# Linear attention (hedgehog) plus dense Mish branch on one core: the first group's layer norm by single tiles, both weight folds ahead of the keys

## The chip, the cores and the metric

One core of a Trainium2 chip runs the whole program in one launch. The metric is device time in microseconds (us), the median of several executions. Besides these, one execution was recorded by the hardware profiler; all rows below are of that one.

## The reference

The input `x` (2048 tokens of 512 numbers, bf16) is layer-normalised, and two branches of the result are added to it:

```python
xn = _layernorm(x)                                  # (x - mean) / sqrt(var + 1e-5)
# A: 32 heads of 16, feature map by two softmaxes
q, k, v = split(xn @ wqkv)
pq, pk = q @ w_phi[h], k @ w_phi[h]
phi_q = concat(softmax(pq), softmax(-pq)); phi_k = concat(softmax(pk), softmax(-pk))
o = (phi_q @ (phi_k.T @ v)) / (phi_q @ sum(phi_k) + 1e-6)
A = o @ wo
# B: dense layer with Mish, F = 1792
h = xn @ w1 + b1
B = (h * tanh(softplus(h))) @ w2
out = x + A + B
```

## The kernel before

The tokens are worked through in four groups of 512, each of four tiles of 128 tokens. The first loop (L445 to L463) does for each group: keys and values (`stage_kv_pair`, two tiles of tokens at a time), queries (`stage_q`), the layer norm of the *next* group (`stage_ln`), the sum of phi_k times v over the tokens (`stage_kvacc`), and the first dense layer with Mish (`stage_h`). A second loop (L479) does the attention output and the second dense layer with the projection.

`stage_ln` takes a group's four tiles on VectorE: statistics (`bn_stats`, `bn_aggr`, L169 and L170), one square root for all four on ScalarE (L171), one reciprocal (L172), four normalising passes to `xn` (L176). TensorE then transposes 16 blocks (L191) into two PSUM tiles `ptr`, and ScalarE copies each to `xnT` (L196).

`fold(src, dst)` multiplies w_phi into the key or query weights ahead of time, so that `pk` and `pq` need one product each. It transposes 16 blocks of the raw weights into PSUM (`ptrw`, L217), ScalarE copies them to `wT` (L223, two buffers), TensorE multiplies with the block-diagonal `Wbd` into four PSUM tiles `pf` (L228), and VectorE casts each to `wkp` or `wqp` (L235). The keys are folded before the group loop; the queries are folded in the first pass of the loop, between the first group's keys and values and its queries (L449).

PSUM is split into three pools: `big` (tag kq, two tiles of two banks: pk, pq, ph, pnd), `bank_v` (two banks: pv, pf, po) and `bank_m` (two banks: ptr, ptrw, pb, pS, pkv, ptro). Buffers of a tag go round: a tile waits until an older one has been read.

The order on each engine is not that of the source: a planner in the framework orders the instructions at build time, by their place in the source and by when it believes them to be ready. `chain` (L139) adds edges that keep ScalarE's Sqrt, Exp and Mish calls in source order, so that the activation tables are switched a fixed number of times. At run time each engine works strictly in that built order. DMAs are issued from the queues of SyncE (SP) and ScalarE (ACT).

Of the kernel before, what the change touches and what calls it, by code (L numbers as in the profile page):

```python
# [8 lines left out]
BF16 = mybir.dt.bfloat16  # L9
FP32 = mybir.dt.float32  # L10

ACT = mybir.ActivationFunctionType
ALU = mybir.AluOpType
# [4 lines left out]
def kernel(  # L18
# [12 lines left out]
    nc = tc.nc  # L31
    P = 128
    S, D, NH, DH, F = 2048, 512, 32, 16, 1792
    NG = 4
    TPG = 4
    NT = NG * TPG
    KT = D // P
# [3 lines left out]
    x2 = A_x.flatten_outer_dims()  # L41
    x_g = x2.rearrange("(g t p) d -> g p t d", t=TPG, p=P)
    x_t = x2.rearrange("(n p) d -> n p d", p=P)
# [4 lines left out]
    w1_v = B_w1.rearrange("(kt p) c -> p kt c", p=P)  # L48
    w2_v = B_w2.rearrange("(ft p) c -> p ft c", p=P)
    wphi_v = A_w_phi.rearrange("(j i) a b -> (i a) j b", j=4)  # L50
    b1_v = B_b1.rearrange("(f p) -> f p", p=P)

    consts = ctx.enter_context(tc.tile_pool(name="consts", bufs=1))
# [5 lines left out]
    xnpool = ctx.enter_context(tc.tile_pool(name="xn", bufs=4))  # L59
    xnTpool = ctx.enter_context(tc.tile_pool(name="xnT", bufs=2))  # L60
    spool = ctx.enter_context(tc.tile_pool(name="small", bufs=4))
# [5 lines left out]
    prep_w = tc.alloc_tile_pool(name="prep_w", bufs=1)  # L67
    xgs = [None] * NG
    xgs[0] = xpool.tile([P, TPG, D], BF16, name="xg")
    for t in range(TPG):  # L70
        nc.sync.dma_start(xgs[0][:, t, :], x_t[t])
    wk_raw = prep_w.tile([P, KT, D], BF16, name="wk_raw")
    nc.scalar.dma_start(wk_raw[:], wqkv_v[:, :, D : 2 * D])
    Wsrc = prep_w.tile([P, 4, DH], BF16, name="Wsrc")
    with nc.allow_non_contiguous_dma(reason="tiny w_phi load"):
        nc.scalar.dma_start(Wsrc[:], wphi_v)
# [2 lines left out]
    wq_raw = prep_w.tile([P, KT, D], BF16, name="wq_raw")  # L79
    nc.scalar.dma_start(wq_raw[:], wqkv_v[:, :, 0:D])  # L80
    b1row = prep_w.tile([FT, P], BF16, name="b1row")
    nc.scalar.dma_start(b1row[:], b1_v)
    w1_sb = wts.tile([P, KT, F], BF16, name="w1_sb")
    nc.sync.dma_start(w1_sb[:, :, 0 : F // 2], w1_v[:, :, 0 : F // 2])
    nc.sync.dma_start(w1_sb[:, :, F // 2 : F], w1_v[:, :, F // 2 : F])
    xgs[1] = xpool.tile([P, TPG, D], BF16, name="xg")
    nc.sync.dma_start(xgs[1][:], x_g[1])
    w2_sb = wts.tile([P, FT, D], BF16, name="w2_sb")
# [5 lines left out]
    ident = consts.tile([P, P], BF16, name="ident")  # L94
    make_identity(nc, ident[:])
    eps_t = consts.tile([P, 1], FP32, name="eps_t")
    nc.gpsimd.memset(eps_t[:], 1e-5)

    mask17 = consts.tile([P, 8, VW], FP32, name="mask17")
    nc.gpsimd.memset(mask17[:], 1.0)  # L100
# [1 line left out]
        out=mask17[:],  # L102
# [8 lines left out]
        out=mask17[:],  # L111
# [13 lines left out]
    wqp = wts.tile([P, KT, D], BF16, name="wqp")  # L125
# [13 lines left out]
    def chain(ins):  # L139

        prev = last_of.get("act")
        last_of["act"] = ins
        if prev is not None:
            tc.add_manual_dep(
                ins.ins,
                prev.ins.name,
                mybir.DependencyInfo(
                    mybir.DependencyClass.NoSync, mybir.DependencyReason.DATA
                ),
                reason="table order",  # L150
            )
# [4 lines left out]
    def bank_v(name):  # L156
        return ps_v.tile([P, 512], FP32, name=name, tag="v")

    def bank_m(name, shape=None, dt=FP32):
        return ps_m.tile(shape or [P, 512], dt, name=name, tag="m")  # L160


    def stage_ln(g):
        xg = xgs[g]
        mv = spool.tile([P, TPG, nc.vector.BN_AGGR_DIM], FP32, name="mv")
        rstd = spool.tile([P, TPG], FP32, name="rstd")
        for t in range(TPG):
            st = spool.tile([P, nc.vector.BN_STATS_DIM], FP32, name="st")
            nc.vector.bn_stats(st[:], xg[:, t, :])  # L169
            nc.vector.bn_aggr(mv[:, t, :], st[:])  # L170
        chain(nc.scalar.activation(rstd[:], mv[:, :, 1], ACT.Sqrt, bias=eps_t[:]))  # L171
        nc.vector.reciprocal(rstd[:], rstd[:])  # L172
        xns = []
        for t in range(TPG):
            xn = xnpool.tile([P, D], BF16, name="xn")
            nc.vector.tensor_scalar(  # L176
                out=xn[:],
                in0=xg[:, t, :],
                scalar1=mv[:, t, 0:1],
                scalar2=rstd[:, t : t + 1],  # L180
                op0=ALU.subtract,
                op1=ALU.mult,
            )
            xns.append(xn)
        xnT = xnTpool.tile([P, KT, 512], BF16, name="xnT")
        for kh in range(2):
            ptr = bank_m("ptr", [P, 2, 512], BF16)
            for t in range(TPG):
                for k in range(2):
                    kt = 2 * kh + k  # L190
                    nc.tensor.transpose(  # L191
                        ptr[:, k, t * P : (t + 1) * P],
                        xns[t][:, kt * P : (kt + 1) * P],
                        ident[:],
                    )
            nc.scalar.copy(xnT[:, 2 * kh : 2 * kh + 2, :], ptr[:])  # L196
        return xnT


# [2 lines left out]
        out=Wbd[:].rearrange("p j (i e) -> p j i e", e=DH),  # L202
        in0=B16b[:, None, :]
# [6 lines left out]
    def fold(src, dst):  # L210
        wTs = []
        for jh in range(2):
            ptr = bank_m("ptrw", [P, 2, 512], BF16)
            for jj in range(2):
                j = 2 * jh + jj
                for kt in range(KT):
                    nc.tensor.transpose(  # L217
                        ptr[:, jj, kt * P : (kt + 1) * P],
                        src[:, kt, j * P : (j + 1) * P],
                        ident[:],  # L220
                    )
            wT = prep_w.tile([P, 2, 512], BF16, name="wT", bufs=2)
            nc.scalar.copy(wT[:], ptr[:])  # L223
            wTs.append(wT)
        for kt in range(KT):
            pf = bank_v("pf")
            for j in range(4):
                nc.tensor.matmul(  # L228
                    pf[:, j * P : (j + 1) * P],
                    lhsT=wTs[j // 2][:, j % 2, kt * P : (kt + 1) * P],  # L230
                    rhs=Wbd[:, j, :],
                    start=True,
                    stop=True,
                )
            nc.vector.tensor_copy(dst[:, kt, :], pf[:])  # L235


    def stage_kv_pair(xnT, pr):
# [47 lines left out]
    def stage_kvacc(g, parts):  # L286
        for s0, s1 in ((0, 3), (3, 6), (6, 8)):
            n = s1 - s0
            pkv = bank_m("pkv", [P, n, 8 * VW])
            for s in range(s0, s1):  # L290
                pl, j = divmod(s, 4)
                for t in range(TPG):
                    ek, v12s = parts[t // 2]
                    nc.tensor.matmul(  # L294
                        pkv[:, s - s0, :],
                        lhsT=ek[:, pl, t % 2, j * P : (j + 1) * P],
                        rhs=v12s[t % 2][:, pl, 8 * j : 8 * j + 8, :],
                        start=(t == 0),
                        stop=(t == TPG - 1),
                    )  # L300
            if g == 0:
                nc.vector.tensor_copy(kvacc[:, s0:s1, :], pkv[:])
            else:
                nc.vector.tensor_tensor(
                    out=kvacc[:, s0:s1, :],
                    in0=pkv[:],
                    in1=kvacc[:, s0:s1, :],
                    op=ALU.add,
                )
# [127 lines left out]

    xnTs = [None] * NG
    acts = [None] * NG
    xnTs[0] = stage_ln(0)  # L440
    fold(wk_raw, wkp)
    pb = bank_m("pb", [P, FT], BF16)
    nc.tensor.transpose(pb[:], b1row[:], ident[0:FT, 0:FT])
    nc.vector.tensor_copy(b1f[:], pb[:])
    for g in range(NG):  # L445
        xnT = xnTs[g]
        parts = [stage_kv_pair(xnT, pr) for pr in range(2)]
        if g == 0:
            fold(wq_raw, wqp)  # L449
            prep_w.release()  # L450
            apool3 = ctx.enter_context(tc.tile_pool(name="act3", bufs=1))
            oTpool = ctx.enter_context(tc.tile_pool(name="oT", bufs=2))
            rpool = ctx.enter_context(tc.tile_pool(name="rden", bufs=4))
            opool = ctx.enter_context(tc.tile_pool(name="o_t", bufs=4))
            ypool = ctx.enter_context(tc.tile_pool(name="y", bufs=2))
        stage_q(g, xnT)
        if g + 1 < NG:
            if g + 1 > 1:
                xgs[g + 1] = xpool.tile([P, TPG, D], BF16, name="xg")
                nc.sync.dma_start(xgs[g + 1][:], x_g[g + 1])  # L460
            xnTs[g + 1] = stage_ln(g + 1)
        stage_kvacc(g, parts)
        acts[g] = stage_h(xnT, apool if g + 1 < NG else apool3)  # L463
# [3 lines left out]
        out=kvv[:, 0:4, :, DH],  # L467
        in0=kvv[:, 0:4, :, DH],
        scalar1=1e-6,
        scalar2=None,  # L470
        op0=ALU.add,
    )
    nc.vector.tensor_tensor(
        out=kvm[:].rearrange("p s (h v) -> p s h v", v=VW),
        in0=kvv,
# [36 lines left out]
```

## Time and profile before

| what | value |
|---|---|
| median of 3 runs | 224.42 us (224.35 to 227.0) |
| the profiled execution, its own time | 226.06 us |
| its span, first to last instruction | 224.3 us |
| TensorE (PE) busy | 197.7 us, 88% |
| VectorE (DVE) busy | 120.4 us, 54% |
| ScalarE (ACT) busy | 101.2 us, 45% |
| mean granted TensorE clock | 0.985 of full |

The span is what the trace covers; the profiled execution's own time is 1.76 us longer than it, and 1.64 us above the median of the runs. An engine's share of busy time is an average over stages that have different limits, so it is to be read stage by stage.

### The profile page before, as it was taken

The page shows a single profiled execution, that of the slowest core. Times are in us where ns is not written, and L with a number is a line of the kernel's source. Part 1 is how long each engine was busy: PE and PEld are TensorE (multiplying, and loading weights), DVE is VectorE, ACT ScalarE, POOL GpSimd, SP SyncE. Part 2 cuts the span into 40 slices and gives each one's busy share as a digit, 9 for nine tenths or more (in the row PEclk, how much of TensorE's full clock was granted, in tenths as well). Part 3 has the DMA queues.
Part 4 walks back from the last instruction along what each step waited for, and adds up shares of the span by engine and source line. Part 5 has one row for each costly group of instructions (what it writes and reads, how often), then busy time and mean ns, then how long its engine had stood idle before and what let it go on. Part 6 is the DMA issues. An engine that isn't in the chain of part 4 may idle for free.

```text
span 224.3 us, 2903 instructions
## 1 busy us (share of the span) xinstructions
PE 197.7 (88%) x1185; PEld 100.1 (45%) x1185; DVE 120.4 (54%) x205; ACT 101.2 (45%) x124; POOL 8.6 (4%) x26
## 2 busy tenths in 40 slices
PE   0089455889999999999999999999999999999993
PEld 0066113346444356443464345564464455446441
DVE  1627598695229992199930998562263145218121
ACT  0263800595789847799469874423003003000200
POOL 2000011000001100011000110000000000000000
PEclk9999967999999999999999999999999999999999
DMA  6999100003000003000020000000131103100011
GB/s 183 380 361 348 43 0 0 0 1 96 0 0 1 0 0 96 0 0 0 3 93 0 3 0 1 0 3 23 41 90 36 47 32 111 46 24 26 23 36 35
DMA packets 12120, 12.25 MB, mean 55 GB/s; under 512 B 1100, under 2 KB 12108, under 8 KB 12108
## 3 DMA queue, kind: packets, MB, share of 16 engines
q1 hardware_dynamic: 10496, 11.01, 15.0%
q10 hardware_dynamic: 1612, 1.07, 1.6%
q8 instruction: 9, 0.15, 0.3%
q14 instruction: 3, 0.02, 0.0%
HBM read 9.98 MB, written 2.10 MB: 54 GB/s over the span
## 4 chain that ended last, share of the span: by engine, by line
PE 70%; ACT 15%; DVE 8%; DMA 2%; issue 2%; SPq 1%; ACTq 0%
PE po L418 22%; PE ph L355 17%; PE po L426 6%; DVE ss L266 5%; PE pkv L294 4%; PE pnd L380 4%; PE pq L319 3%; PE pv L258 3%; PE pk L243 3%; ACT eq L328 2%; DMA xg<-in_A_x_dram 2%; ACT L171 2%; PE pS L333 2%; PE ptr L191 2%; ACT ek L252 2%
## 5 line engine op out<-in xcount | busy, mean ns | idle before, releaser
L355 PE MATMUL ph<-xnT,w_sb 128*128 128x512 bf16 x224 | 55.5, 379 | 1.7 <-ACT act L365 1.7
L418 PE MATMUL po<-w_sb,act 128*128 128x512 bf16 x224 | 54.4, 379 | 0.0
L365 ACT ACTIVATE act<-ph,b1f 128x512 bf16<-128x512 f32 x56 | 35.1, 685 | 19.7 <-PE ph L355 19.6
L434 DVE TENSOR_TENSOR y<-po,xg 128x512 bf16<-128x512 f32 x16 | 11.1, 692 | 46.8 <-PE po L426 46.8
L355 PEld LDWEIGHTS <-w_sb 128*128 128x128 bf16 x224 | 21.6, 98 | 26.8 <-issue 3.1
L408 ACT COPY oT<-ptro 128x1024 bf16<-128x1024 bf16 x8 | 7.7, 1015 | 53.5 <-PE ptro L403 53.5
L266 DVE TENSOR_REDUCE ss<-ek 128x64 f32<-128x1024 bf16 x16 | 18.7, 1214 | 24.2 <-ACT ek L252 24.2
L418 PEld LDWEIGHTS <-act 128*128 128x128 bf16 x224 | 21.2, 98 | 22.2
L340 DVE TENSOR_TENSOR eqT<-pS,eq 128x512 bf16<-128x512 f32 x32 | 20.6, 689 | 3.2 <-PE pS L333 3.1
L258 PE MATMUL pv<-wv,xnT 128*128 128x512 bf16 x64 | 17.1, 404 | 4.8 <-DVE v_260 L274 4.8
L319 PE MATMUL pq<-xnT,wqp 128*128 128x512 bf16 x64 | 16.6, 405 | 1.0 <-ACT ek L252 1.0
L426 PE MATMUL po<-wo_sb,oT 128*128 128x512 bf16 x64 | 17.2, 380 | 0.0
L243 PE MATMUL pk<-wkp,xnT 128*128 128x512 bf16 x64 | 15.9, 387 | 0.0
L191 PE MATMUL ptr<-ident,xn 128*128 128x128 bf16 x64 | 6.1, 242 | 10.7 <-DVE xn L176 10.7
L327 ACT ACTIVATE eq<-pq 128x1024 bf16<-128x1024 f32 x8 | 8.2, 1028 | 14.9 <-PE pq L319 14.3
L169 DVE BATCH_NORM_STATS2 st<-xg 128x6 f32<-128x512 bf16 x16 | 10.5, 675 | 5.3 <-DMA xg<-in_A_x_dram 5.3
L258 PEld LDWEIGHTS <-xnT 128*128 128x128 bf16 x64 | 6.5, 102 | 13.2 <-issue 6.4
L333 PE MATMUL pS<-eq,B16b 128*128 128x512 bf16 x32 | 11.5, 378 | 0.9 <-ACT eq L328 0.9
L391 DVE TENSOR_TENSOR o_t<-pnd,rd 128x512 bf16<-128x512 f32 x16 | 11.1, 692 | 0.6
L319 PEld LDWEIGHTS <-wqp 128*128 128x128 bf16 x64 | 6.6, 105 | 9.3 <-issue 2.9
L191 PEld LDWEIGHTS <-xn 128*128 128x128 bf16 x64 | 4.4, 106 | 12.6 <-DVE xn L176 11.9
L196 ACT COPY xnT<-ptr 128x1024 bf16<-128x1024 bf16 x8 | 7.7, 1015 | 5.0 <-PE ptr L191 5.0
(96 smaller groups left out, 203.7 us busy)
## 6 DMA issues: line engine op xcount, KB each, us to landing
xg<-in_A_x_dram SPq DMA_DIRECT2D x7, 512.0 KB, 4.0
out_dram<-y SPq DMA_DIRECT2D x16, 128.0 KB, 1.7
w_sb<-in_B_w_dram SPq DMA_DIRECT2D x2, 896.0 KB, 7.5
w_sb<-in_B_w_dram SPq DMA_DIRECT2D x1, 1792.0 KB, 13.4
wk_raw<-in_A_wqkv_dram ACTq DMA_DIRECT2D x1, 512.0 KB, 4.2
xg<-in_A_x_dram SPq DMA_DIRECT2D x4, 128.0 KB, 4.3
wq_raw<-in_A_wqkv_dram ACTq DMA_DIRECT2D x1, 512.0 KB, 5.9
wv<-in_A_wqkv_dram SPq DMA_DIRECT2D x1, 512.0 KB, 6.5
```

The source lines that it names most:

```text
L191: nc.tensor.transpose(ptr[:, k, t * P : (t + 1) * P], xns[t][:, kt * P : (kt + 1) * P], ident[:],)
L243: nc.tensor.matmul(pk[:, tt, :], lhsT=xnT[:, kt, tok0 : tok0 + P], rhs=wkp[:, kt, :], start=(kt == 0), stop=(kt == KT - 1),)
L258: nc.tensor.matmul(pv[:], lhsT=xnT[:, kt, tok0 : tok0 + P], rhs=wv[:, kt, :], start=(kt == 0), stop=(kt == KT - 1),)
L266: nc.vector.reduce_sum(ss[:], ek[:, :, tt, :].rearrange("p s (h e) -> p s h e", e=DH), axis=AX.X,)
L319: nc.tensor.matmul(pq[:, jj, :], lhsT=wqp[:, kt, j * P : (j + 1) * P], rhs=xnT[:, kt, :], start=(kt == 0), stop=(kt == KT - 1),)
L333: nc.tensor.matmul(pS[:], lhsT=B16b[:], rhs=eq[:, 1 - pl, jj, :], start=True, stop=True,)
L340: nc.vector.tensor_tensor(out=eqT[:, pl * 4 + j, gs], in0=pS[:], in1=eq[:, pl, jj, :], op=ALU.mult,)
L355: nc.tensor.matmul(ph[:, ff, :], lhsT=w1_sb[:, kt, f * P : (f + 1) * P], rhs=xnT[:, kt, :], start=(kt == 0), stop=(kt == KT - 1),)
L365: nc.scalar.activation(act[:, f, :], ph[:, ff, :], ACT.Mish, bias=b1f[:, f : f + 1])
L391: nc.vector.tensor_tensor(out=o_t[:].rearrange("p (a h e) -> p a h e", a=2, e=DH), in0=nd[:, :, :, 0:DH], in1=rd[:, :, :, None].to_broadca ...
L418: nc.tensor.matmul(po[:], lhsT=act[:, f, ts], rhs=w2_sb[:, f, :], start=(f == 0), stop=False,)
L426: nc.tensor.matmul(po[:], lhsT=oT[:, j, ts], rhs=wo_sb[:, j, :], start=False, stop=(j == 3),)
```

## The change

Three things change. The first group's layer norm runs tile by tile (statistics, square root, reciprocal and normalising pass of one tile, then its transposes); the later groups keep one square root for four tiles, but all groups now transpose two token tiles into one `ptr` and copy `xnT` by halves of the tokens instead of halves of the features. A one-element Sqrt ahead of the first layer norm and a one-element Exp behind it (`warm`) make ScalarE load these tables there. Both folds stand ahead of the group loop, their `pf` tiles come from `bank_m` instead of `bank_v`, and every second `pf` is cast by ScalarE instead of VectorE. Besides, the first `x` tiles are loaded by two DMAs instead of four, `b1row` goes through SP's queue, and `eps_t` is set by VectorE.

```diff
-    for t in range(TPG):
-        nc.sync.dma_start(xgs[0][:, t, :], x_t[t])
+    x0 = x2[0 : TPG * P].rearrange("(t p) d -> p t d", p=P)
+    nc.sync.dma_start(xgs[0][:, 0:2, :], x0[:, 0:2, :])
     wk_raw = prep_w.tile([P, KT, D], BF16, name="wk_raw")
     nc.scalar.dma_start(wk_raw[:], wqkv_v[:, :, D : 2 * D])
+    nc.sync.dma_start(xgs[0][:, 2:4, :], x0[:, 2:4, :])
...
-    nc.scalar.dma_start(b1row[:], b1_v)
+    nc.sync.dma_start(b1row[:], b1_v)
...
-    nc.gpsimd.memset(eps_t[:], 1e-5)
+    nc.vector.memset(eps_t[:], 1e-5)
+    warm = consts.tile([P, 1], FP32, name="warm")
...
+        step = 1 if g == 0 else TPG
+        for t0 in range(0, TPG, 2):
+            ptr = bank_m("ptr", [P, KT, 2 * P], BF16)
+            for t in range(t0, t0 + 2):
+                if t % step == 0:
+                    for u in range(t, t + step):
+                        st = spool.tile([P, nc.vector.BN_STATS_DIM], FP32, name="st")
+                        nc.vector.bn_stats(st[:], xg[:, u, :])
+                        nc.vector.bn_aggr(mv[:, u, :], st[:])
+                    us = slice(t, t + step)
+                    chain(
+                        nc.scalar.activation(
+                            rstd[:, us], mv[:, us, 1], ACT.Sqrt, bias=eps_t[:]
+                        )
+                    )
+                    nc.vector.reciprocal(rstd[:, us], rstd[:, us])
+                xn = xnpool.tile([P, D], BF16, name="xn")
...
+                for kt in range(KT):
                     nc.tensor.transpose(
-                        ptr[:, k, t * P : (t + 1) * P],
-                        xns[t][:, kt * P : (kt + 1) * P],
+                        ptr[:, kt, (t - t0) * P : (t - t0 + 1) * P],
+                        xn[:, kt * P : (kt + 1) * P],
                         ident[:],
                     )
-            nc.scalar.copy(xnT[:, 2 * kh : 2 * kh + 2, :], ptr[:])
+            nc.scalar.copy(xnT[:, :, t0 * P : (t0 + 2) * P], ptr[:])
...
-            pf = bank_v("pf")
+            pf = bank_m("pf")
...
-            nc.vector.tensor_copy(dst[:, kt, :], pf[:])
+            if kt % 2 == 0:
+                nc.vector.tensor_copy(dst[:, kt, :], pf[:])
+            else:
+                nc.scalar.copy(dst[:, kt, :], pf[:])
...
+    chain(nc.scalar.activation(warm[:], eps_t[:], ACT.Sqrt))
     xnTs[0] = stage_ln(0)
+    chain(nc.scalar.activation(warm[:], eps_t[:], ACT.Exp))
     fold(wk_raw, wkp)
+    fold(wq_raw, wqp)
...
         if g == 0:
-            fold(wq_raw, wqp)
             prep_w.release()
```

## Rows read from the trace of the kernel before

**Rows 1.** The page's part 1: busy time, share of the span and instructions of each engine.
```profile
PE 197.7 (88%) x1185; PEld 100.1 (45%) x1185; DVE 120.4 (54%) x205; ACT 101.2 (45%) x124; POOL 8.6 (4%) x26
```
**Rows 2.** Busy time by stretch (windows): stretch, its length, engines, granted clock, DMA share.
```profile
24.60:29.75 5.15, 0.36 (x2) 0.08 (x1) 4.34 (x6) 2.61 (x3) 0.86 (x2) 1.00 0.00 0
29.75:37.00 7.25, 4.21 (x20) 1.82 (x20) 7.25 (x9) 0.00 (x0) 0.86 (x2) 0.76 0.00 0
37.00:45.00 8.00, 7.05 (x31) 3.15 (x29) 5.55 (x13) 3.50 (x4) 0.00 (x0) 0.79 0.00 0
...
61.20:89.90 28.70, 27.78 (x161) 13.67 (x160) 18.83 (x28) 22.36 (x28) 1.78 (x4) 1.00 0.06 19
```
**Rows 3.** Who waited for whom from 18.9 to 61.2 us: total, times, longest.
```profile
ACT eq L327 <- PE pq L319: 14.3, 1, 14.3
PE pv L258 <- DVE v_260 L274: 4.8, 1, 4.8
PE pf L228 <- DVE v_296 L274: 2.1, 1, 2.1
```
**Rows 4.** Timeline of loads and the first layer norm: start, duration, engine, line, operation.
```profile
0.81 1.79 SPq L71 DMA_DIRECT2D xg<-in_A_x_dram  x4
3.01 0.69 DVE L169 BATCH_NORM_STATS2 st<-xg 128x6 f32<-128x512 bf16 x1 [3.01 <-DMA xg<-in_A_x_dram]
5.54 0.69 DVE L169 BATCH_NORM_STATS2 st<-xg 128x6 f32<-128x512 bf16 x1 [1.84 <-DMA xg<-in_A_x_dram]
6.15 0.16 DVE L170 BATCH_NORM_AGGREGATE mv<-st 128x2 f32<-128x6 f32 x1
7.39 0.69 DVE L169 BATCH_NORM_STATS2 st<-xg 128x6 f32<-128x512 bf16 x1 [0.42 <-DMA xg<-in_A_x_dram]
8.38 1.28 ACT L171 ACT_TABLE_LOAD   x1 [8.38 <-DVE mv L170]
9.68 0.30 ACT L171 ACTIVATE rstd<-mv,eps_t 128x4 f32<-128x4 f32 x1
10.01 0.18 DVE L172 RECIPROCAL rstd<-rstd 128x4 f32<-128x4 f32 x1 [1.71 <-ACT rstd L171]
11.33 0.41 DVE L176 TENSOR_SCALAR xn<-xg,mv,rstd 128x512 bf16<-128x512 bf16 x1
```
**Rows 5.** Timeline of the key fold and the first products, and of two later groups' first keys.
```profile
13.29 1.93 PE L217 MATMUL ptrw<-ident,wk_raw 128*128 128x128 bf16 x16 [0.35 <-ACT xnT L196]
14.34 1.93 ACT L223 COPY wT<-ptrw 128x1024 bf16<-128x1024 bf16 x2 [0.19 <-PE ptrw L217]
15.41 0.61 PE L228 MATMUL pf<-Wbd,wT 128*128 128x128 bf16 x4 [0.19 <-ACT wT L223]
17.34 1.29 DVE L235 CAST wkp<-pf 128x512 bf16<-128x512 f32 x2 [0.39 <-PE pf L228]
18.91 1.06 PE L243 MATMUL pk<-wkp,xnT 128*128 128x512 bf16 x2
20.05 0.81 PE L243 MATMUL pk<-wkp,xnT 128*128 128x512 bf16 x3
22.14 1.28 ACT L251 ACT_TABLE_LOAD   x1
61.20 1.89 PE L243 MATMUL pk<-wkp,xnT 128*128 128x512 bf16 x8
89.94 1.89 PE L243 MATMUL pk<-wkp,xnT 128*128 128x512 bf16 x8
```
**Rows 6.** VectorE's longest jobs of the first group, by shape, to 61.2 us: total, mean ns.
```profile
L340 DVE TENSOR_TENSOR eqT<-pS,eq 128x512 bf16<-128x512 f32 x8 | 5.1, 688 | 1.9 <-PE pS L333 1.9
L266 DVE TENSOR_REDUCE ss<-ek 128x64 f32<-128x1024 bf16 x4 | 4.7, 1213 | 2.3 <-ACT ek L252 2.3
L272 DVE RECIPROCAL rk<-ss 128x64 f32<-128x64 f32 x4 | 1.9, 522 | 0.0
L274 DVE TENSOR_TENSOR v_308<-pv,rk 128x1024 bf16<-128x1024 f32 x1 | 1.2, 1220 | 0.0
```

More of the change, by code (lines that the diff above doesn't have):

```diff
@@ L81 @@
     b1row = prep_w.tile([FT, P], BF16, name="b1row")
-    nc.scalar.dma_start(b1row[:], b1_v)
+    nc.sync.dma_start(b1row[:], b1_v)
     w1_sb = wts.tile([P, KT, F], BF16, name="w1_sb")
-    nc.sync.dma_start(w1_sb[:, :, 0 : F // 2], w1_v[:, :, 0 : F // 2])
-    nc.sync.dma_start(w1_sb[:, :, F // 2 : F], w1_v[:, :, F // 2 : F])
+    F2 = F // 2
+    nc.sync.dma_start(w1_sb[:, :, 0:F2], w1_v[:, :, 0:F2])
+    nc.sync.dma_start(w1_sb[:, :, F2:F], w1_v[:, :, F2:F])
     xgs[1] = xpool.tile([P, TPG, D], BF16, name="xg")
@@ L166, in stage_ln @@
         rstd = spool.tile([P, TPG], FP32, name="rstd")
[L167 to L184, printed above, removed]
@@ L185, in stage_ln @@
-        xnT = xnTpool.tile([P, KT, 512], BF16, name="xnT")
[L186 to L190, printed above, removed]
+        xnT = xnTpool.tile([P, KT, 512], BF16, name="xnT")
+        step = 1 if g == 0 else TPG
[15 more added lines that the diff above has]
+                xn = xnpool.tile([P, D], BF16, name="xn")
+                nc.vector.tensor_scalar(
+                    out=xn[:],
+                    in0=xg[:, t, :],
+                    scalar1=mv[:, t, 0:1],
+                    scalar2=rstd[:, t : t + 1],
+                    op0=ALU.subtract,
+                    op1=ALU.mult,
+                )
+                for kt in range(KT):
```

## The prediction

> **What bounds the kernel now.** I began with the busy shares [rows 1]: TensorE has matmuls in flight for 88% of the span, so the 26.6 us in which it has none are what an edit of order can win. The windows say where they are. A later group (61.2 to 89.9) leaves TensorE 0.9 us of 28.7 unused [rows 2]; from the first group's second half, 24.6 to 45, it is busy for 0.36 + 4.21 + 7.05 of 20.4 us, and at granted clocks of 0.76 and 0.79 for the last 15 of them, a mix of the 2.4 and 1.2 GHz levels [rows 2]. From the first keys at 18.91 to the next group's at 61.20 are 42.3 us; from 61.20 to 89.94, for the same work without folds, 28.7 [rows 5]. So group 0 costs 13.6 us too much, and 18.9 us go by before its first product.
>
> Who waits in it [rows 3]: ScalarE stands 14.3 us for `pq`; TensorE 4.8 us for a PSUM bank that holds `pv` until VectorE has written `v12`, and then 2.1 us with the query fold, whose `pf` needs the same two banks and stands behind the values in the source. VectorE is busy for all of 29.75 to 37.00 [rows 2]. The reader should see a queue: queries wait for the folded weights, those for a bank, the bank for VectorE's work on values.
>
> **Start and layer norm.** The last `x` tile's statistics start at 7.39, after a wait for its load; then come the table load (1.28), the root (0.30), the reciprocal (0.18) and four normalising passes, of which the last starts at 11.33 and takes 0.41, so the last `xn` is there at 11.74 [rows 4]. The table load leaves the path: `warm` needs only `eps_t`, and ScalarE has nothing to compute before 8.38 [rows 4].
>
> The Trainium skill ("ScalarE: Activation LUTs", What ACT_TABLE_LOAD costs) counts a drain of 1.38 us on top of the 1.28 for every switch. No row here shows it, as the root starts at 9.68 behind a load that ends at 9.66 [rows 4]; by the page 1.4 us more would be won, and I leave them out.
>
> The loads: single tiles let statistics start at 3.01 and 5.54, the last at 7.39 [rows 4]. The pair 0 and 1 now lands as one, between these first two times; I take 4.9, near the second, as its later half decides. Tiles 2 and 3 are issued before the value weights and not behind three other issues: between 5.5 and 7.4, taken as 6.3. From 4.9 VectorE needs for each tile 0.69 + 0.16 + 0.18 + 0.41 = 1.44 us by its rows, some 1.35 with the overlap of neighbours, and the root of one tile runs on ScalarE beside the next one's statistics. Four tiles end at about 10.3, 1.4 earlier than 11.74. Three more reciprocals and roots are in it. If the second pair lands at 7.4 the end moves little, since VectorE gets to it at 7.6.
>
> Behind the last `xn` comes a chain of single steps, all on rows 5 (16 transposes 1.93, two copies 1.93, four products 0.61, two casts 1.29): last transposes 0.5, `xnT` copy 1.0, eight transposes of raw key weights 1.0, `wT` copy 1.0, four products 0.6, cast 0.7, some 0.1 of hand-over each: 5.4, so the first `pk` at about 15.9, say 16.0, where 18.91 stood. The later three `pf` follow at half the cast time, on two engines: a ScalarE cast of this shape isn't in the trace; its bounds are half of a 128x1024 copy (0.5) and a VectorE cast (0.69, half of 1.29), I take 0.69. It costs the path nothing, as `pf` steps alternate. Bounds of the first `pk`: 18.9 (nothing won) and 11.5, if the raw key weights are transposed while the layer norm runs. Before, they waited for the `xnT` copy and not for their load [rows 5], so I keep to 16.0.
>
> The small Exp behind the norm costs 1.28 + some 0.3 on ScalarE beside VectorE's last tile; if it slips between the copies it costs up to 1.6. It replaces the load at 22.14 [rows 5], which stood ahead of the first `ek`. `b1row` now queues on SP behind the value weights; its use comes after both folds. `eps_t` on VectorE is one tiny write ahead of any load: nothing, and 0.2 if badly placed.
>
> **The query fold, moved.** It takes with it 16 transposes (1.93 for 16), 16 products (four times 0.61) and the four casts. The casts are a chain of copies of some 7 us for one fold (2.0 transposes, 2.0 copies, 3 for four `pf` on two banks), so `wqp` is complete at about 23.5. Under it TensorE has pk, pk, pv, pv of the first tiles, 32 matmuls, 6.9 us at 0.216 each (eight take 1.89 less the overhang of the last, 61.20 [rows 5]), and the fold's own work: it is covered up to some 26 us. The wait of 14.3 for `pq` goes; what is late next is TensorE itself. `ek` queues behind the fold's copies on ScalarE, so `ss` starts at about 22.5 and not at 25.41. VectorE then has for the group 4.7 + 1.9 + 4 x 1.2 + 5.1 = 16.5 us [rows 6], with four `xn` and a few casts 20, and is through at 43; TensorE isn't before 48, so VectorE doesn't set the end.
>
> **Sum.** First `pk` 16.0; a group as the later ones run, 28.7 [rows 5]; fold work that now falls behind the first `pk`, 16 transposes 1.9, 16 products and the last of the key fold some 2.5, less 0.4 at the faster steps: 4.0; matmuls at the low clock. The first two keys took 0.43 a step, 1.06 for two, and by 20.05 a step is 0.22 [rows 5], that is 1.2 and then 2.4 GHz. TensorE's dense work starts later now in relation to the first `pk`, so more of it falls to the lower level: between 1.0 (as before) and 4, taken as 2.0. That is 50.7 for the next group's first key in place of 61.2: 10.5 us won. Everything behind 61.2 stays: same instructions, and the halves by tokens in place of features copy as many elements, which I price at nothing; the cover is the `ph` work around it, without which 16 transposes and a copy, 2 us per group, could show.
>
> Against the profiled execution that is 226.06 - 10.5 = 215.6, and 213.8 of span; this execution lay 1.64 above the median, so the median should be 224.42 - 10.5 = 213.9.
>
> **Rivals.**
> 1. *Faster start.* The planner fits the key fold under the layer norm: first `pk` at 11.5. For it: TensorE and ScalarE are free until 10. Against: it didn't do so before. 4.5 more: 209.4.
> 2. *Casts behind values.* VectorE works in built order. If the planner puts the `wqp` casts behind both pairs of `ss`, `rk`, `v12` (10.7 us), `wqp` comes at 34 rather than 23.5; TensorE is covered to 26 and has half the values to do, so it loses about 6: 220. For it: before, that was the order; against: its cause was the bank, and the fold now precedes them in the source.
> 3. *The order doesn't change.* The planner goes by its own times; if `pf` still comes late, only the start is won: 224.4 - 2.9 = 221.5.
> 4. *Slower: the clock.* Before, the lower level came after 5.15 us with hardly a matmul [rows 2]. The new start is thin: two-bank rounds with a cast between every four small products, and transposes in ones and fours. If the clock then stays at the lower level through group 0, each us of its 27.8 us of matmuls costs one more; from 10.5 us on it eats the whole gain. Held through the group: 213.9 + 27.8 - 2 = 239.7. Against: from 18.91 it came up within two us in a stretch that also had waits.
>
> The Trainium skill speaks for this one ("TensorE: Matmul & The Clock Gate", A second HAM failure mode: psum-queue depth-cycling): matmul groups that cycle through PSUM banks with small pauses can make the clock fall and rise again and again. The first fold here had such pauses and rows 5 show the clock rising all the same.
>
> **How the numbers follow.** Forecast (211 to 217) 0.66; rival 1 (207 to 211) 0.13; rival 2, 0.11, about half of it below 219.9; rival 3, 0.06; rival 4, 0.04. A measurement tells about 2% (4.5 us) from no change: faster means below 219.9. Faster 0.66 + 0.13 + 0.07 = 0.86; same 0.10; slower 0.04. The range: below, rival 1's 209.4 less some low-clock time, 208.0; above, late loads and the clock's 4 us with part of rival 2, 219.0.
>
> **What the new profile would show.** Right: a table load on ScalarE before 5 us; last `xn` near 10.3; first `pk` near 16 with pauses under 1 us behind it; no wait of ScalarE for `pq` above 4 us; no stretch of TensorE between 16 and 50 without work for over 2 us; the second group's first `pk` at 49 to 53 and 163 us from there to the end, as before. Wrong: `pq` still behind the fourth `v12`; steps of 0.43 well past 22 us; the loads of `x` later than 7.4; or later groups longer than 28.7 us, which I have not priced.

## The result, and the profile after

The changed kernel takes 212.4 us (median of four runs, 212.14 to 212.47), the kernel before in the same session 225.3 (224.35 to 227.0): a ratio of 0.9418, 95% interval 0.935 to 0.9485. The forecast was 213.9, range 208 to 219. The profiled execution took 212.4 with a span of 210.7; that of before 226.06 and 224.3. Medians and ratios below leave out one slow execution each of e3 and e5, and e5's is the profiled one (granted clock 0.95 from 13.6 us on), so TensorE's steps in its trace are some 4% too long.

First the page's part 1 of the changed kernel (busy time, share of the span, instructions), to be read beside [rows 1]:

```profile
PE 193.6 (92%) x1185; PEld 98.0 (47%) x1185; DVE 117.8 (56%) x205; ACT 104.5 (50%) x133; POOL 8.6 (4%) x25
```

TensorE is without matmuls for 17.1 us in place of 26.6, and its busy time fell by 4.1 with the same 1185 matmuls: fewer of them ran at the lower clock. The windows of the changed kernel put a place to it (length, busy time by engine, granted clock, DMA): the first group from its first `pk` to the next group's, and the rest.

```profile
17.57:47.32 29.75, 28.61 (x188) 14.70 (x186) 26.82 (x50) 23.20 (x30) 1.83 (x4) 1.00 0.28 90
47.32:210.70 163.38, 157.38 (x945) 77.98 (x943) 84.21 (x134) 72.81 (x90) 5.27 (x12) 1.00 0.08 26
```

Between the same two marks before, 18.91 and 61.20, lie 42.3 us [rows 5]; now 29.75, at full clock, with 1.1 us unused. From the second mark to the end are 163.4 us, before 163.1 (224.3 - 61.2): the later groups, with their `xnT` copied by tokens, neither won nor lost. So 12.5 of the 13.6 us came from group 0 and 1.3 from the start; 0.3 went behind. (Eight `pv` products of group 0, 1.7 us at full clock, now run ahead of the first mark, so the split counts them as a gain of group 0 and as a cost of the start.)

The timeline of the changed kernel (start, duration, engine, line, operation) answers to [rows 4] and [rows 5]:

```profile
2.44 1.28 ACT L449 ACT_TABLE_LOAD   x1 [2.44 <-issue]
4.43 1.29 DVE L178 BATCH_NORM_STATS2 st<-xg 128x6 f32<-128x512 bf16 x2 [3.50 <-DMA xg<-in_A_x_dram]
5.84 0.29 ACT L182 ACTIVATE rstd<-mv,eps_t 128x1 f32<-128x1 f32 x1 [1.90 <-DVE mv L179]
6.55 0.69 DVE L178 BATCH_NORM_STATS2 st<-xg 128x6 f32<-128x512 bf16 x1 [0.75 <-DMA xg<-in_A_x_dram]
8.20 0.41 DVE L188 TENSOR_SCALAR xn<-xg,mv,rstd 128x512 bf16<-128x512 bf16 x1
8.73 1.06 DVE L188 TENSOR_SCALAR xn<-xg,mv,rstd 128x512 bf16<-128x512 bf16 x3
11.77 0.63 PE L267 MATMUL pv<-wv,xnT 128*128 128x512 bf16 x1
13.29 1.01 ACT L229 COPY wT<-ptrw 128x1024 bf16<-128x1024 bf16 x1 [0.27 <-PE ptrw L223]
14.12 1.32 PE L267 MATMUL pv<-wv,xnT 128*128 128x512 bf16 x4
15.28 0.50 PE L234 MATMUL pf<-Wbd,wT 128*128 128x128 bf16 x6
15.81 0.59 ACT L244 CAST wkp<-pf 128x512 bf16<-128x512 f32 x1 [1.51 <-PE pf L234]
16.01 0.69 DVE L178 BATCH_NORM_STATS2 st<-xg 128x6 f32<-128x512 bf16 x1 [5.64 <-DMA xg<-in_A_x_dram]
16.45 0.38 PE L234 MATMUL pf<-Wbd,wT 128*128 128x128 bf16 x4 [0.46 <-ACT wkp L244]
16.62 0.67 DVE L242 CAST wkp<-pf 128x512 bf16<-128x512 f32 x1
17.35 0.38 PE L234 MATMUL pf<-Wbd,wT 128*128 128x128 bf16 x4 [0.52 <-DVE wkp L242]
17.57 1.03 PE L252 MATMUL pk<-wkp,xnT 128*128 128x512 bf16 x4
18.43 1.06 PE L223 MATMUL ptrw<-ident,wq_raw 128*128 128x128 bf16 x16
23.66 1.89 PE L328 MATMUL pq<-xnT,wqp 128*128 128x512 bf16 x8
47.32 1.89 PE L252 MATMUL pk<-wkp,xnT 128*128 128x512 bf16 x8
```

Four things are to be seen. The queries follow the keys at 23.66, and ScalarE's wait for `pq`, 14.3 us in [rows 3], isn't among the waits any more. The layer norm does *not* run tile by tile: the planner put the statistics of tiles 2 and 3 ahead of the first `xn`, so VectorE waits 0.75 us for a load at 6.55, though the first root is out at 6.13; by these rows, what the norm won is the loads and the table. `pv` of the first tiles, eight products, stands between the steps of the key fold, from 11.77. Not all of it fills gaps: the second `wT` copy is done at 14.30, but the `pf` products that read it start at 15.28, behind four `pv` at 14.12. And the first `pk` waits for a cast at 16.62 that stands on VectorE behind a statistic of the *second* group, whose load came at 16.0: an idle time of 5.64 us that TensorE paid for in part.

### The profile page after: what moved, and what is told of

The parts are those of the page before. It is cut to its first block, busy times and chain, and to the rows that moved or that the text cites. A ratio compares the mean times of both kernels' runs of the same rounds, so it can differ in the third digit from the quotient of the medians.

```text
span 210.7 us, 2908 instructions
## 1 busy us (share of the span) xinstructions
PE 193.6 (92%) x1185; PEld 98.0 (47%) x1185; DVE 117.8 (56%) x205; ACT 104.5 (50%) x133; POOL 8.6 (4%) x25
## 3 DMA queue, kind: packets, MB, share of 16 engines
q1 hardware_dynamic: 10492, 11.02, 15.9%
## 4 chain that ended last, share of the span: by engine, by line
PE 71%; ACT 10%; DVE 9%; DMA 7%; issue 1%; SPq 0%; ACTq 0%
PE po L427 23%; PE ph L364 18%; PE po L435 7%; DVE ss L275 5%; DMA xg<-in_A_x_dram 5%; PE pkv L303 4%; PE pnd L389 4%; PE pk L252 3%; PE pv L267 3%; PE pS L342 3%; DMA wk_raw<-in_A_wqkv_dram 2%; ACT ek L261 2%; PE ptro L412 2%; ACT eq L337 2%; PE pq L328 2%; PE ptr L197 1%
## 5 line engine op out<-in xcount | busy, mean ns | idle before, releaser
L328 PE MATMUL pq<-xnT,wqp 128*128 128x512 bf16 x64 | 15.1, 379 | 1.6 <-ACT ek L261 1.5
L435 PEld LDWEIGHTS <-oT 128*128 128x128 bf16 x64 | 5.6, 98 | 8.9 <-ACT oT L417 3.2
L389 PEld LDWEIGHTS <-eqT 128*128 128x128 bf16 x128 | 7.9, 98 | 3.8 <-DVE o_t L400 2.4
L389 PE MATMUL pnd<-kvm,eqT 128*128 128x136 bf16 x128 | 9.6, 223 | 0.0
```

The lines of the kernel that those rows point to most:

```text
L328: nc.tensor.matmul(pq[:, jj, :], lhsT=wqp[:, kt, j * P : (j + 1) * P], rhs=xnT[:, kt, :], start=(kt == 0), stop=(kt == KT - 1),)
L389: nc.tensor.matmul(pnd[:, j // 2, (j % 2) * 136 : (j % 2) * 136 + 136], lhsT=eqT[:, pl * 4 + j, tok0 : tok0 + P], rhs=kvm[:, pl * 4 + j, : ...
L435: nc.tensor.matmul(po[:], lhsT=oT[:, j, ts], rhs=wo_sb[:, j, :], start=False, stop=(j == 3),)
```

## The experiments

Twelve kernels ran in three sets of four; within a set they shared the chip and the runs of the kernel before (226.19, 226.36 and 226.31 us). So times are compared inside a set, and ratios to before across sets. The changed kernel itself ran in none of these sets; its ratio is 0.9418 (0.935 to 0.9485), and a difference of 1% or less from it lies at the edge of the intervals or inside them. "Theory A": the place of the query fold in the order is what cost. "B": the start brings most. "C": the shared banks were the cost. "D": the second group's late load held up the start. "E": the lower clock at the start costs little. "F": the second engine for the casts shortens the rounds, that is the four products and their cast that take turns in two banks.

| kernel | us | ratio to before, 95% |
|---|---|---|
| e1 query fold moved, nothing else | 213.63 | 0.9431 (0.9399 to 0.9464) |
| e2 `pf` in `bank_m`, nothing else | 224.77 | 0.9919 (0.9889 to 0.9949) |
| e3 layer norm, tables, loads alone | 222.77 | 0.9853 (0.9803 to 0.9903) |
| e4 both folds as changed, no norm part | 214.53 | 0.9467 (0.9431 to 0.9504) |
| e5 changed, second group's x early | 210.73 | 0.9315 (0.9273 to 0.9356) |
| e6 changed, `pf` back in value banks | 221.46 | 0.9810 (0.9765 to 0.9855) |
| e7 e6 with the second group's x early | 212.20 | 0.9377 (0.9336 to 0.9419) |
| e8 changed, 60 extra products | 217.52 | 0.9621 (0.9579 to 0.9663) |
| e9 e5, 85 extra products, order pinned | 210.49 | 0.9318 (0.9278 to 0.9357) |
| e10 changed, no tables ahead | 213.41 | 0.9461 (0.9416 to 0.9506) |
| e11 e4 with the second group's x early | 214.82 | 0.9514 (0.9467 to 0.9561) |
| e12 e5, all casts on VectorE | 210.44 | 0.9299 (0.9257 to 0.9342) |

**e1: the fold's place alone.** The kernel before with one line moved:

```diff
     fold(wk_raw, wkp)
+    fold(wq_raw, wqp)
...
         if g == 0:
-            fold(wq_raw, wqp)
             prep_w.release()
```

> The kernel before with one edit: the query fold stands ahead of the group loop; its pf tiles stay in the banks of pv and VectorE alone casts. Theory A (the place in the order is what costs: pq waited behind the values): the 14.3 us wait of ScalarE for pq goes, 8 to 11 us won, ratio 0.952 to 0.965. Theory B (the start with its layer norm and tables brings most): under 3 us, 0.987 or above. Theory C (the shared banks are the cost): under 4 us, since pf and pv still share two banks, 0.982 or above.

Measured 213.63, 12.6 us off: more than A's upper end, and nearly all that the whole change brings. Its timeline on TensorE:

```profile
16.20 1.06 PE L217 MATMUL ptrw<-ident,wq_raw 128*128 128x128 bf16 x8
18.69 0.38 PE L243 MATMUL pk<-wkp,xnT 128*128 128x512 bf16 x1
25.63 3.62 PE L319 MATMUL pq<-xnT,wqp 128*128 128x512 bf16 x15
48.72 1.89 PE L243 MATMUL pk<-wkp,xnT 128*128 128x512 bf16 x8
```

`pf` and `pv` still share two banks and VectorE still casts alone, and the queries start at 25.63 where 37.10 stood; the next group starts at 48.72 where 61.20 stood. A stands, C falls.

**e2: the banks alone.** `pf = bank_m("pf")` in the kernel before, nothing else.

> The kernel before with one edit: pf takes its PSUM from bank_m; the query fold stays behind the first keys and values in the source. Theory A: some of the fold moves up, but the planner still puts its last products behind the second pair of values, which wait for VectorE; 0 to 5 us won, ratio 0.978 to 1.0. Theory C: the waits for the value banks (4.8 + 2.1) and for pq (14.3) go, 8 to 11 us won, 0.952 to 0.965. Theory B: nothing, 1.0.

Measured 224.77, 1.4 us off. The built order had kept the wait. VectorE's timeline in this kernel:

```profile
29.56 2.33 DVE L266 TENSOR_REDUCE ss<-ek 128x64 f32<-128x1024 bf16 x2
31.81 0.95 DVE L272 RECIPROCAL rk<-ss 128x64 f32<-128x64 f32 x2
32.69 2.29 DVE L274 TENSOR_TENSOR v<-pv,rk 128x1024 bf16<-128x1024 f32 x2
34.89 1.28 DVE L235 CAST wqp<-pf 128x512 bf16<-128x512 f32 x2
```

The casts of `wqp` stand behind both pairs of values and start at 34.89; ScalarE waits 12.8 us for `pq` against 14.3 [rows 3]. This is rival 2 of the forecast, in another kernel than it was written for.

**e3 and e4: the two halves of the change.** e3 is the changed kernel with `fold` and its calls as before; e4 is e1 with `pf` in `bank_m` and every second cast on ScalarE.

> The changed kernel with its folds set back (place, banks and VectorE casts as before), so the layer norm, tables and loads alone. Theory A: only the earlier start, 1.3 to 3 us won, ratio 0.987 to 0.994, and the wait for pq stays. Theory B: 8 us or more, below 0.965. Theory C: as A.

> The kernel before with the folds of the changed one (ahead of the loop, pf in bank_m, casts on two engines), without the layer norm, tables and loads. Theory A: 9.5 to 12 us won, ratio 0.947 to 0.958, the change less the 1.3 to 3 us of the start. Theory B: under 5 us, 0.978 or above. Theory C: as A, and clearly more than with the fold moved alone.

e3 takes 3.4 us off, a little over the 1.3 to 3 expected, and e4 11.7. Theory B falls. e4 is 0.9 us *slower* than e1 in the same set: own banks and a second engine for the casts together brought nothing here. With the two folds in two banks, the query weights' transposes wait for the key fold's casts (19.86 in e4's trace, 16.20 in e1's above). The norm part is worth 3.4 us alone; on top of the folds the ratios of changed kernel and e4 leave 0.5%, 1.1 us, which is inside their intervals.

**e5: the second group's load early.** To test what held up the first `pk`:

```diff
     nc.sync.dma_start(b1row[:], b1_v)
+    xgs[1] = xpool.tile([P, TPG, D], BF16, name="xg")
+    nc.sync.dma_start(xgs[1][:], x_g[1])
     w1_sb = wts.tile([P, KT, F], BF16, name="w1_sb")
...
     nc.sync.dma_start(w1_sb[:, :, F2:F], w1_v[:, :, F2:F])
-    xgs[1] = xpool.tile([P, TPG, D], BF16, name="xg")
-    nc.sync.dma_start(xgs[1][:], x_g[1])
```

> The changed kernel with one edit: the load of the second group's x is issued ahead of the w1 loads on SP's queue. Theory D (the first pk at 17.57 was late because VectorE, in its built order, stood on the second group's statistics until their load came at 16.0, with the first cast of wkp behind them): first pk at 16.2 to 16.8 and 0.8 to 1.3 us off, 211.1 to 211.6 if the changed kernel is at 212.4. Rival (the chain of copies and transposes alone sets 17.57): no change, 212.0 to 212.8.

Measured 210.73, ratio 0.9315 against 0.9418: some 1% better, a little more than D said; the intervals just touch, and that of e12 below lies just clear. Its first `pk` stands at 16.61, where D had it. VectorE's timeline in e12, which has the same load order, shows the block gone:

```profile
11.56 1.29 DVE L178 BATCH_NORM_STATS2 st<-xg 128x6 f32<-128x512 bf16 x2 [1.40 <-DMA xg<-in_A_x_dram]
13.05 0.39 DVE L207 TENSOR_TENSOR Wbd<-B16b,Wsrc 128x512 bf16<-128x512 bf16 x1
13.36 1.28 DVE L178 BATCH_NORM_STATS2 st<-xg 128x6 f32<-128x512 bf16 x2
16.09 2.51 DVE L241 CAST wkp<-pf 128x512 bf16<-128x512 f32 x4 [1.24 <-PE pf L234]
```

All four statistics are done before the first `pf` and the casts run in one piece. There the first `pk` is at 17.28, hardly earlier, yet the next group starts at 46.26 and not at 47.32: part of the gain lies behind the first `pk`, where the casts no longer have statistics between them. So D's place is right and its mark, the first `pk`, was too narrow. What else holds the first `pk` shows in TensorE's timelines of e12, of e5, and of e7 (below), in which `pv` stands behind the keys:

```profile
14.50 1.45 PE L264 MATMUL pv<-wv,xnT 128*128 128x512 bf16 x4
15.78 0.50 PE L234 MATMUL pf<-Wbd,wT 128*128 128x128 bf16 x6
17.28 0.38 PE L249 MATMUL pk<-wkp,xnT 128*128 128x512 bf16 x1
...
13.99 1.07 PE L267 MATMUL pv<-wv,xnT 128*128 128x512 bf16 x4
14.89 0.50 PE L234 MATMUL pf<-Wbd,wT 128*128 128x128 bf16 x6
16.61 0.61 PE L252 MATMUL pk<-wkp,xnT 128*128 128x512 bf16 x2
...
15.39 0.38 PE L249 MATMUL pk<-wkp,xnT 128*128 128x512 bf16 x1
20.40 1.89 PE L264 MATMUL pv<-wv,xnT 128*128 128x512 bf16 x8
```

From the last `xn` to the first `pk` it is 7.8 us in the changed kernel, 7.1 in e12, 6.6 in e5 and 5.75 in e7 (last `xn` at 9.79, 10.17, 9.99 and 9.64). By these traces the statistics make 0.7 to 1.2 of the 2.0 us between the changed kernel and e7, and the `pv` products ahead of `pf`, with the lower clock in which they ran, 0.9 to 1.4.

**e6 and e7: value banks again.** The changed kernel with `pf` in `bank_v` and VectorE casts, without (e6) and with (e7) e5's early load.

> The changed kernel with pf back in the banks of pv and all casts on VectorE; the folds stay ahead of the loop and the layer norm stays by tiles. Theory A (the place does it; own banks and the second engine bring nothing, since ptrw and pf of both folds now share two banks): 0 to 1.2 us faster than the changed kernel, 211.2 to 212.4. Rival (own banks and two engines are part of the gain): 1 us slower or more, 213.4 or above.

> Both edits: pf in the value banks with VectorE casts, and the second group's x loaded ahead of w1. Theories A and D together: first pk at 15 to 16, 209.5 to 211.3, the fastest. If D is false: as the kernel with pf in the value banks.

e6 came out where the rival said, 9 us slower than the changed kernel, though mostly not by the banks themselves but by the order built with them. ScalarE's and TensorE's timelines in e6:

```profile
33.76 1.28 ACT L182 ACT_TABLE_LOAD   x1
38.55 1.19 PE L339 MATMUL pS<-eq,B16b 128*128 128x512 bf16 x2 [0.25 <-DVE eqT L346]
41.84 0.30 ACT L182 ACTIVATE rstd<-mv,eps_t 128x4 f32<-128x4 f32 x1 [6.79 <-DVE mv L179]
42.15 1.28 ACT L371 ACT_TABLE_LOAD   x1
44.28 1.89 PE L197 MATMUL ptr<-ident,xn 128*128 128x128 bf16 x16 [4.54 <-DVE xn L188]
```

And three of its windows (length, PE, PEld, ACT, DVE and POOL busy, granted clock, DMA):

```profile
36.00:40.00 4.00, 2.67 (x6) 0.48 (x5) 3.93 (x8) 0.00 (x0) 0.00 (x0) 0.82 0.01 2
40.00:44.00 4.00, 0.00 (x0) 0.00 (x0) 4.00 (x14) 2.13 (x3) 0.00 (x0) 0.50 0.00 0
44.00:48.00 4.00, 3.50 (x28) 3.15 (x30) 1.19 (x4) 3.37 (x6) 0.00 (x0) 0.50 0.37 118
```

The second group's root needs all four tiles' statistics. Here the planner had put three of the four statistics early and left the fourth until behind `eqT` (the queries' features, scaled by `pS`), at 40.47. The root then waits until 41.84, the Mish table and every `act` stand behind it on ScalarE, the normalising passes behind it on VectorE, and TensorE, whose next work in order is the transposes of that `xn`, stops for 4.54 us. It was at the lower level before it stopped: the granted clock of 36 to 40 is 0.82, in a stretch of single `pS` products with pauses of some 0.2 us for VectorE, and the last two of them took 1.19 us. Behind the stop it runs on at half the clock and takes 1.89 us for 16 transposes. With the load early (e7) the statistics are all early, that wait is gone, and 9.3 us with it. The early load is the only edit between the two. e7's first `pk` came at 15.39, inside the 15 to 16 expected, but its time is outside the 209.5 to 211.3: it is 1.5 us behind e5, and by the ratios 0.8% behind e12, from which only the banks of `pf` set it apart. So in this setting the own banks seem to help (the two intervals just touch), where e4 against e1 said the opposite. What the banks are worth depends on the order the planner builds around them.

**e8 and e9: the clock of the start.** 60 products on the identity ahead of the layer norm in the changed kernel; then 85 in e5, with the third group's statistics tied behind `eqT` so that VectorE's and ScalarE's orders equal e5's.

```diff
+    wu = big("wu")
+    for i in range(85):
+        nc.tensor.matmul(wu[:, 0, 0:P], lhsT=ident[:], rhs=ident[:], start=True, stop=True)
     xnTs[0] = stage_ln(0)
```

> The changed kernel with 60 extra 128x128 products on the identity ahead of the layer norm, whose result nobody reads, so that TensorE is active from 1.5 us on. They add work and no output. Theory E (the low clock to 15 us cost little, because TensorE there waits for copies and casts): at most 0.8 us off, 211.6 to 212.6. Rival (as the forecast priced it: the low clock costs the start 2 us): 1.5 to 2.5 us off, 209.9 to 210.9.

> The kernel with the second group's x loaded early, plus 85 extra 128x128 products on the identity ahead of the layer norm (more work, no output), and the third group's statistics pinned behind the first group's eqT, so that VectorE's and ScalarE's built orders are the same as without the products. Theory E (the lower clock up to the first pk costs little, TensorE waits for copies and casts there): 0 to 0.6 us off the 210.7 of that kernel, 210.1 to 210.9. Rival (the forecast's 2 us for the lower clock were real, only lay ahead of the first pk): 1 to 2 us off, 208.7 to 209.7. If TensorE's clock falls again in the gap ahead of the transposes, it shows as steps of 0.107 there, and the run tells nothing.

e8 was 5 us slower, which neither theory had: the extra work on TensorE changed what the planner believed, and it put all four statistics of the second group, and their wait for the load, ahead of VectorE's first cast. TensorE then stood 4.4 us for `wkp`. That is e5's mechanism at a higher price, and tells nothing of the clock. e9, with the order held, is 210.49 against 210.73. But the clock did not stay up; its windows from 8 to 12 and from 12 to 16:

```profile
8.00:12.00 4.00, 2.14 (x26) 1.61 (x26) 2.54 (x12) 3.61 (x7) 0.00 (x0) 0.96 1.09 355
12.00:16.00 4.00, 3.78 (x24) 2.35 (x23) 3.04 (x11) 2.11 (x3) 0.00 (x0) 0.61 1.05 376
```

TensorE's timeline at their border:

```profile
11.32 0.70 PE L232 MATMUL ptrw<-ident,wk_raw 128*128 128x128 bf16 x8 [0.73 <-ACT xnT L211]
12.67 1.06 PE L232 MATMUL ptrw<-ident,wk_raw 128*128 128x128 bf16 x8 [0.22 <-issue]
```

The first eight transposes took 0.70 us, not 1.01, the second eight 1.06: half of the fold was still at the lower level. By its own condition the run decides nothing. The traces of e12 and e5 above say a little: from the start of the four `pv` to that of the `pf` behind them it is 1.28 and 0.90 us, 0.32 and 0.22 a product, as e12's clock was still low for some of them and e5's was not. So the lower clock does cost some tenths of a us on this path; what a full clock would bring in time stays open.

**e10: no tables ahead.** The changed kernel without the two one-element activations.

> The changed kernel without the two one-element activations, so that the Sqrt table loads when the first tile's statistics are there and the Exp table ahead of the first ek. By the forecast's step (the 1.28 us load leaves the path): 0.8 to 1.6 us slower than 212.4, 213.2 to 214.0. Rival (the start isn't bound by the norm but by VectorE's statistics of the second group, which wait for their load to 16.0): within 0.4 us of it, 212.0 to 212.8.

Measured 213.41, ratio 0.9461 against 0.9418: about 1 us slower (the intervals overlap), inside the first expectation, but not for its reason. ScalarE's timeline:

```profile
2.45 1.28 ACT L182 ACT_TABLE_LOAD   x1 [2.45 <-issue]
6.07 0.29 ACT L182 ACTIVATE rstd<-mv,eps_t 128x1 f32<-128x1 f32 x1 [2.34 <-DVE mv L179]
...
21.41 1.28 ACT L260 ACT_TABLE_LOAD   x1
22.70 1.02 ACT L260 ACTIVATE ek<-pk 128x1024 bf16<-128x1024 f32 x1
```

The Sqrt table is loaded at 2.45 all the same. Before, the load waited for the statistics [rows 4]; here it doesn't, without `warm`. Of the edits left that touch the root (`eps_t` set by VectorE, one tile per root), the second isn't needed for it: in e6 above, the load ahead of a root of four tiles ran at 33.76 and the root at 41.84. That leaves `eps_t`, which no run tests alone. What `warm` hides is the Exp load, ahead of the first `ek`: TensorE's wait of `pq` for `ek` is 1.3 us here and 0.4 in the changed kernel. The order moved as well: here both of ScalarE's casts of `wqp` stand ahead of the second `ek`, there one of them stands behind it. How much of the 1 us is the load and how much the order was not separated.

**e11 and e12: the norm part and the second engine, once the load is early.** e11 is e4 with the early load; e12 is e5 with all casts on VectorE.

> The kernel with the fold part alone, plus the second group's x loaded ahead of w1. Theory D (the late load hid part of the layer norm's gain): without the norm part there is less to unblock, 0.2 to 1.0 us off its 214.5, 213.5 to 214.3, and the norm part is worth 2.3 to 3.5 us once the load is early (against the 210.7 of the changed kernel with that edit). Rival (the norm part is worth the same with or without it, some 1.5 to 2 us): 212.2 to 212.8.

> The changed kernel with the second group's x loaded early and all casts of the folds on VectorE; pf stays in bank_m. Theory F (the second engine for the casts shortens each two-bank round): 0.5 to 1.5 us slower than 210.7, 211.2 to 212.2. Rival (casts are off the path): 210.4 to 211.0.

e11 is 214.82: no gain over e4 (0.9514 and 0.9467, the intervals overlap), outside D's figure by half a us. Without the norm part nothing stood behind that load. e12 is 210.44, no slower than e5: theory F falls. In the same set e12 and e11 are 4.4 us apart, of which the cast engine accounts for nothing by e5 and e12: so much is the norm part worth once the load is early, more than the 2.3 to 3.5 expected and against 1.1 to 3.4 without it.

e12, e5 and e9 are the best kernels of the study: some 1% under the changed one, 7% under the one before.

## Why the forecast came out, point by point

**The mechanism** was right: queries waited for the fold, the fold for a place behind the values. e1 shows it by one moved line; e2 shows that the place, not the bank, carries it, and that it is VectorE's order where the bank is free. So the bank, which the forecast had as a link of its queue and as the cause of the old order (rival 2), isn't needed for the wait. The forecast gave the casts on two engines no price ("It costs the path nothing"), and e12 agrees. Own banks it gave none either; e4 has them at nothing and e7 against e12 at 0.8%.

**The first `pk`**, 16.0 in the forecast (its 10.3 and 5.4 make 15.7 and not 15.9, a slip of 0.2), came at 17.57. The layer norm ended earlier than priced (9.79 for 10.3; the pairs of `x` landed at 4.43 and 6.55, priced 4.9 and 6.3). What failed is the step from the last `xn` to `pk`, 5.4 in the sum and 7.8 in the trace: it counted transposes, copies and casts as if VectorE and TensorE were free between them. VectorE's built order had the second group's statistics there, and their load, which the sum never looked at; TensorE's had `pv` ahead of `pf`. In e7, where neither stands there, the step takes 5.75 us, though its products ran at full clock by then. In time, moving the load is worth 1.7 us (e5); `pv` has to run somewhere, and e7 is no faster for having it later.

**Fold work behind the first `pk`**, 4.0, and **the low clock**, 2.0, were both too large: 29.75 less 28.7 leaves 1.0 for the two. The fold's price came from rows at the lower clock. The transposes and products of the query fold ran at steps of 0.056, 16 in 1.06, at full clock: some 1.8 us for 32. Against that, eight `pv` products, 1.7 us at full clock, were done ahead of `pk`, which the forecast did not have. Behind the first `pk` four products took 1.03, full steps: the lower level fell on the start, on the key fold's steps, which were priced from rows at that level, and on the `pv` between them, which were not priced there. Sum: 5.0 too much here, 1.6 too little at the start; the next group's first `pk` came at 47.32 for 50.7, outside the 49 to 53 that the forecast had named as a sign of being right. The errors had opposite signs, which is why the total was near; that part of the hit is luck. By gain it was less near: 10.5 us forecast, 12.9 measured against the kernel before in the same session.

**What stays behind** was right: 163.4 us for 163.1, so the new `xnT` halves cost nothing that shows.

**The rivals.** Rival 1 didn't come: TensorE's first `wk_raw` transpose starts at 10.97, behind the norm and a wait for the `xnT` copy, and what was put between the fold's steps is `pv`. Rival 2 and rival 3 didn't come here; rival 2 is what e2 does. Rival 4 didn't come: the pauses of 0.46 and 0.52 us between the key fold's last products left the clock at 1.00. In e6 it came, and not as in [rows 2], where 5.15 us with hardly a matmul lie ahead of it: it came in the stretch of single `pS` products, before TensorE stopped.

**The table load and the pauses.** The drain of 1.38 us that the Trainium skill counts with every table load ("ScalarE: Activation LUTs", What ACT_TABLE_LOAD costs) shows in no trace here: in e10 `ek` starts at 22.70, behind a load that ends at 22.69. What the Trainium skill says of matmul groups that cycle through PSUM banks, that small pauses between them can make the clock fall and rise again and again ("TensorE: Matmul & The Clock Gate", A second HAM failure mode: psum-queue depth-cycling), did not show in the changed kernel, by the clock in the windows above. In e6 the trace agrees with the fall: the granted clock of 0.82 came in a stretch of such pauses.

## What to carry to other kernels

Where a planner or the source fixes each engine's order, read a wait by what stands *ahead of the releaser on its own engine*: a bank, a second engine or a table brings little while a cast sits behind work of another stage. Look for early work of the next stage (statistics, prefetches) that was put into a gap and waits for a load there, as it blocks everything behind it; moving that load is cheap. And a change that leaves work alone can still move the order by what the planner believes, so judge a part by its trace, not by the sum of the parts.

## What the runs showed of the hardware

Table loads took 1.28 us in every trace, with nothing behind them, and some loads didn't wait for the operand of their activation (e10, 2.45 against 6.07; e6, 33.76 against 41.84).

TensorE's granted clock fell in e9 from 0.96 to a mean of 0.61 in a stretch in which it was busy for 3.78 of 4.0 us; the stretch ahead had 2.14 of 4.0, behind 85 back-to-back products. There the lower level fell on dense work behind a half-idle stretch. In e6 the granted clock was already 0.82 between 36 and 40 us, where TensorE was busy for 2.67 us with single products, ahead of its long stop.

A cast of 128x512 from PSUM took 0.59 us on ScalarE and 0.67 on VectorE, in the same kernel.
